# Two more two-level products in layer one's first down stage and one in layer two's, and evictions moved to ScalarE and GpSimd

## The chip, the cores and the metric

The kernel runs on one core of one Trainium2 chip. The metric is the time of one execution on the device in microseconds (us). The median of three runs of the kernel before is 1431.98 us.

## The reference: what is computed

An input `x` of 2048 tokens by 1024 features in bf16 passes through two blocks, twice with the same weights:

```python
x = x + A(layernorm(x), wqkv, wo)                 # linear attention, 32 heads
x = x + B(layernorm(x), w_gate, w_up, w_down)     # ((x @ w_gate) * (x @ w_up)) @ w_down
x = x + A(layernorm(x), wqkv, wo)
x = x + B(layernorm(x), w_gate, w_up, w_down)
```

`w_gate` and `w_up` are 1024x3584, `w_down` is 3584x1024. One A and one B together are a layer here: layer one and layer two. The change concerns the last product of B, by `w_down`.

## The kernel before, in words

**Order of work.** The program is recorded first: each operation goes into a list with the memory that it reads and writes, and each engine then runs its own operations in the order in which they were recorded. Waits between engines come from the memory they share. All transfers are issued by SyncE (SP) from one queue, in recorded order too. So an operation that waits holds up everything recorded behind it on its engine. SBUF is one big tensor named `arena`, PSUM is one named `ps`; that is why all rows read `arena<-ps` and the like.

**Block B** runs in two passes (`ps_` 0 and 1) of 1024 tokens. A pass has a gate/up stage, which leaves h in SBUF, and a down stage (`down`), in which h (1024x3584) is multiplied by `w_down` (3584x1024). The down stage is a Strassen-Winograd product: seven products, named "1" to "7", each of 512 tokens by 1792 by 512, in the order that `DPROD` gives, over sums of blocks of h and of `w_down`.

**One-level product** (matmuls L2109): four token tiles `t`, each with 14 matmuls of 512 columns into one PSUM bank, then the eviction of that bank. In a stage of layer one's first pass VectorE also prepares sums of weight blocks there, one quarter a tile.

**Two-level product** (`two_level`, matmuls L2017): the same scheme once more inside the product, seven sub-products (1, 5, 6, 7, 2, 3, 4 in order of time) of 7 matmuls of 256 columns for each of two token halves, 98 matmuls. Beside the matmuls it needs
- token sums: `a_sums` makes four sums of blocks of h, each 128x1792 on VectorE (three into a buffer, one in place);
- weight sums: `r_sums` makes four sums of weight blocks, 128x1792 each, in layer one's first pass; they are stored in DRAM (`d_scratch`) and loaded again in the later passes;
- seeds (L2021): ScalarE copies a partial product from one PSUM bank to another, where later sub-products add to it;
- a copy into SBUF of sub-product 5 on ScalarE (L2035), and joins (L2024) in which VectorE adds that copy to another partial product in PSUM.

The table `DTWO` says which products of a pass run at two levels: before, none in layer one's first pass, 5, 3 and 2 in layer two's first, and 5, 3, 2 and 4 in the second pass of both.

**Fillers.** `EX` is a list of sums for the next two-level product, from which `ex_pop` records a few at fixed places; `x_pop` does the same with sums of x and of weights for the next gate/up stage (T1 to T4, each 2048 wide, are four of them); `ring_issue` issues the next weight load; `stash` stores rows of x in DRAM to free their place, and they are loaded again later. `pro_step` records, inside product 3, the first matmuls (L1668, L1593) of the stage that follows.

**Evictions.** `stt` (L844) is VectorE's scaled add of a PSUM bank and a term in SBUF; `tt` (L841) is VectorE's sum of two SBUF operands; `evict_x` lets ScalarE copy the bank to SBUF, scaled (L2060), and GpSimd add the rest (L2062). `evict5` is the eviction of product 5, two terms a tile. In layer two `final` issues the output transfer of a finished piece.

## Time and profile before

| | us |
|---|---|
| runs, lowest to highest (three) | 1431.52 to 1432.1 |
| median | 1431.98 |
| profiled execution | 1432.3 |
| its span, first to last instruction | 1430.6 |
| TensorE busy | 1420.2 |
| VectorE, ScalarE, GpSimd busy | 1167.1, 733.5, 314.6 |
| down stages of layer one, passes 0 and 1, about | 403 to 488, 651 to 730 |
| down stages of layer two, passes 0 and 1, about | 1108 to 1191, 1348 to 1428 |

The granted TensorE clock is full speed throughout. A row of the timeline gives start, duration, engine, line, operation, tensors, shape, how many instructions are put together, and in brackets the idle time before with what ended it. A row of the groups ends with the busy time in us and the mean in ns of one instruction. A row of the windows gives a stretch of time, and for each engine the busy time and the number of instructions.

### The profile page before, as it was taken

Reading aid. Unit: us, or ns where it says so; the run is one execution under the profiler, and the core shown is the slowest. Engines: PE = TensorE matmul, PEld = TensorE weight load, DVE = VectorE, ACT = ScalarE, POOL = GpSimd, SP = SyncE. Lnnn points to the kernel's source line nnn. Section 1 sums busy time; section 2 is a strip of 40 time slices with the busy share of each in tenths; the row PEclk is TensorE's granted clock in tenths of the full one; section 3 lists DMA queues with packets and bytes.
Section 4 is the critical chain, followed back from the end, with each engine's and each line's share of the span. In section 5 each row is a group of like instructions: output and inputs, shape, how many; then the busy total and the mean of one; then the engine's idle time right before and its main releaser. Section 6 shows DMA issues by size and latency. Waiting matters only on the chain.

```text
span 1430.6 us, 22386 instructions
## 1 busy us (share of the span) xinstructions
PE 1420.2 (99%) x8332; PEld 809.8 (57%) x8388; DVE 1167.1 (82%) x2012; ACT 733.5 (51%) x1538; POOL 314.6 (22%) x321
## 2 busy tenths in 40 slices
PE   9999999999999999999999999999999999999999
PEld 4444444555544555554764444456666477666658
DVE  7878887888879799878778878779877877777886
ACT  4752367767621255552256523667776116777521
POOL 5644632000013000003334346301000400000160
PEclk9999999999999999999999999999999999999999
DMA  6316867987878899985998067589976699788668
GB/s 235 106 28 182 182 137 195 289 294 251 290 253 286 296 324 303 293 260 171 262 355 220 27 178 162 137 229 273 287 253 200 224 299 317 255 261 265 207 187 259
DMA packets 393997, 330.15 MB, mean 231 GB/s; under 512 B 178337, under 2 KB 342049, under 8 KB 393377
## 3 DMA queue, kind: packets, MB, share of 16 engines
q1 hardware_dynamic: 393888, 328.72, 77.0%
q8 instruction: 66, 1.08, 0.3%
q14 instruction: 43, 0.34, 0.1%
HBM read 238.49 MB, written 66.58 MB: 213 GB/s over the span
## 4 chain that ended last, share of the span: by engine, by line
PE 95%; DVE 2%; ACT 1%; issue 1%; POOL 1%; DMA 0%; SPq 0%; ACTq 0%
PE ps L1593 27%; PE ps L1668 18%; PE ps L2109 14%; PE ps L2017 8%; PE ps L1499 8%; PE ps L1401 8%; PE ps L1167 6%; PE ps L971 4%; PE ps L981 2%; PE ps L1413 1%; ACT arena L493 0%; DVE arena L841 0%; DMA arena<-in_A_x_dram 0%; PE ps L1441 0%; ACT arena L473 0%
## 5 line engine op out<-in xcount | busy, mean ns | idle before, releaser
L841 DVE TENSOR_TENSOR arena<-arena 128x512 f16<-128x512 f16 (+9 forms) x780 | 480.5, 644 | 76.4 <-ACT arena L1712 45.1
L1593 PE MATMUL ps<-arena 128*128 128x512 f16 x1808 | 446.8, 379 | 0.6 <-ACT ps L1623 0.6
L1668 PE MATMUL ps<-arena 128*128 128x256 f16 x2324 | 312.1, 273 | 0.7 <-ACT arena L1712 0.6
L844 DVE SCALAR_TENSOR_TENSOR arena<-ps,arena 128x512 f16<-128x512 f32 (+2 forms) x392 | 259.9, 685 | 38.8 <-PE ps L1593 16.3
L1668 PEld LDWEIGHTS ps<-arena 128*128 128x128 f16 (+1 forms) x2324 | 226.4, 98 | 104.0 <-DVE ps L1687 3.8
L1593 PEld LDWEIGHTS ps<-arena 128*128 128x128 f16 (+1 forms) x1808 | 176.5, 98 | 141.7 <-ACT ps L1623 1.1
L2062 POOL TENSOR_TENSOR arena<-arena 128x512 f32<-128x512 f32 x56 | 87.4, 1565 | 596.5 <-ACT arena L2060 591.5
L2109 PE MATMUL ps<-arena 128*128 128x512 f16 (+1 forms) x941 | 205.7, 379 | 0.6
L1598 ACT ACTIVATE arena<-ps 128x512 f16<-128x512 f32 x224 | 134.0, 598 | 91.8 <-PE ps L1593 89.8
L2109 PEld LDWEIGHTS ps<-arena 128*128 128x128 f16 x952 | 93.2, 98 | 111.5
L1684 ACT COPY ps<-ps 128x256 f32<-128x256 f32 x220 | 81.0, 368 | 79.8 <-PE ps L1668 73.4
L1687 DVE TENSOR_TENSOR ps<-ps,arena 128x256 f32<-128x256 f32 x220 | 92.3, 428 | 34.5 <-PE ps L1668 18.3
L2017 PE MATMUL ps<-arena 128*128 128x256 f16 (+1 forms) x1078 | 119.0, 273 | 0.1
L1401 PE MATMUL ps<-arena 128*128 128x512 bf16 x499 | 114.1, 379 | 0.7
L2017 PEld LDWEIGHTS ps<-arena 128*128 128x128 f16 x1078 | 104.9, 98 | 13.9 <-DVE ps L2024 0.4
L1499 PE MATMUL ps<-arena 128*128 128x512 bf16 x500 | 110.7, 379 | 0.6
L2060 ACT ACTIVATE arena<-ps 128x512 f32<-128x512 f32 x48 | 28.7, 597 | 132.6 <-PE ps L2109 132.6
L1167 PE MATMUL ps<-arena 128*128 128x512 bf16 (+1 forms) x412 | 94.7, 379 | 0.8 <-DVE ps L1171 0.3
L1307 POOL TENSOR_TENSOR arena<-arena 128x1024 f16<-128x1024 f32 x32 | 80.0, 2501 | 69.5 <-DVE arena L1305 62.3
L1623 ACT COPY ps<-ps 128x512 f32<-128x512 f32 x112 | 64.2, 573 | 50.2 <-PE ps L1668 44.8
L1006 POOL TENSOR_TENSOR arena<-arena 128x512 f32<-128x512 f32 x60 | 73.6, 1245 | 69.4 <-DVE arena L1096 33.6
L1499 PEld LDWEIGHTS ps<-arena 128*128 128x128 f16 x512 | 50.1, 98 | 59.8
(80 smaller groups left out, 1262.0 us busy)
## 6 DMA issues: line engine op xcount, KB each, us to landing
arena<-w_scratch SPq DMA_DIRECT2D x84, 512.0 KB, 5.2
arena<-sp_scratch SPq DMA_DIRECT2D x56, 512.0 KB, 5.8
arena<-t_scratch SPq DMA_DIRECT2D x27, 896.0 KB, 5.8
arena<-in_B_w_down_dram SPq DMA_DIRECT2D x18, 896.0 KB, 6.2
w_scratch<-arena SPq DMA_DIRECT2D x28, 512.0 KB, 6.0
sp_scratch<-arena SPq DMA_DIRECT2D x28, 512.0 KB, 4.4
arena<-in_B_w_gate_dram SPq DMA_DIRECT2D x42, 256.0 KB, 5.1
arena<-in_B_w_up_dram SPq DMA_DIRECT2D x42, 256.0 KB, 3.4
```

Source lines behind the costliest of these rows:

```text
L841: P.add("dve", lambda e: e.tensor_tensor(out=out, in0=a, in1=b, op=op), rd=rd, wr=wr, prd=prd)
L844: P.add("dve", lambda e: e.scalar_tensor_tensor(out=out, in0=a, scalar=sc, in1=b, op0=ALU.mult, op1=op1), rd=rd, wr=wr, prd=prd)
L1167: P.add("pe", lambda e: [e.matmul(psb(bank), x[:, k, :], w[:, k, :], start=(start and k == 0), stop=(k == 3), skip_group_check=True) for k ...
L1401: return [e.matmul(psb(bank), xr[:, t, j * 128:(j + 1) * 128], pk[:, h, t, :], start=(t == 0), stop=(t == NST - 1)) for t in range(NST)]
L1499: return [e.matmul(psb(bank), xnT[:, g, i * 128:(i + 1) * 128], wp[:, g, dh * 512:(dh + 1) * 512], start=(dh == 0 and g == 0), stop=(g == ...
L1593: P.add("pe", lambda e: [e.matmul(psb(bank), w[:, k, :], x[:, k, :], start=(start and k == 0), stop=(k == 3), skip_group_check=True) for k ...
L1598: P.add("act", lambda e: e.activation(t, psb(bank), AF.Copy, scale=SG), prd=[bank], wr=r)
L1668: P.add("pe", lambda e: [e.matmul(psb(bank)[:, 256 * half:256 * half + 256], w[:, k, :], xx[:, k, :], start=(start and k == 0), stop=(k == ...
L1687: P.add("dve", lambda e: e.tensor_tensor(out=psb(dst[c])[:, 256:512], in0=lo, in1=c5, op=ALU.add), prd=[bk], rd=rc5, pwr=[dst[c]])
L2017: P.add("pe", lambda e: [e.matmul(psb(bank)[:, 256 * half:256 * half + 256], a[:, k, :], w[:, k, :], start=(start and k == 0), stop=(k == ...
L2062: P.add("pool", (lambda k2, x: lambda e: e.tensor_tensor(out=rtmp[k2], in0=rtmp[k], in1=x, op=ALU.add))(k2, x), rd=rx + rr(k), wr=rr(k2))
L2109: return [e.matmul(psb(bank), hv[:, 7 * hf + k, t * 128:(t + 1) * 128], w[:, k, :], start=(start and hf == 0 and k == 0), stop=(hf == 1 an ...
```

## The change

- In layer one's first pass products 5 and 3 run at two levels too (`l2j`). Their seven weight operands come straight from the loaded weights and from the sums that `r_sums` makes at the time. For product 5 all the sums but one weight sum (which is put into product 4) are recorded inside product 6; those for product 3 inside product 5. The fourth token sum of each goes to GpSimd.
- In layer two's first pass product 4 runs at two levels; the order of products becomes 1672453, as in the second passes. The fillers T1 to T4 move to products 2 and 4, ahead of the others.
- `evict5` (all four passes) was two VectorE operations a tile. It is now one ScalarE copy out of PSUM and two GpSimd adds.
- In layer one's first pass the third of VectorE's three evictions of product 6 becomes ScalarE's and GpSimd's.
- The sums in DRAM are stored in three parts and laid out contiguously; rows 8 to 15 of x are stashed rather than 11 to 15, to make room.

```diff
-        DPROD = {(True, 0): "1274653", (True, 1): "1672453", (False, 0): "1674253", (False, 1): "1672453"}
-        DTWO = {(True, 0): "", (True, 1): L2D, (False, 0): "532", (False, 1): L2D}
+        DPROD = {(True, 0): "1274653", (True, 1): "1672453", (False, 0): "1672453", (False, 1): "1672453"}
+        DTWO = {(True, 0): "", (True, 1): L2D, (False, 0): L2D, (False, 1): L2D}
...
-                ts = zip([("t1", t1), ("t2", t2), ("t3", t3), ("t4", t4)], has("1"))
-                return [x for a in ts for x in a] + has("3") + has("2") + has("5")
+                return [("t1", t1), ("t2", t2), ("t3", t3), ("t4", t4)] + has("1") + has("3") + has("2") + has("5")
...
+                l2j = "53" if first and ps_ == 0 else ""
...
+                            lambda: op(blk[1, 0], blk[0, 0], blk[1, 0], ALU.subtract, "pool" if l2j else "dve")]
...
                 def evict5(t, bank):
-                    pb = psb(bank)
                     xs, rx = xq(1, 1, t)
-                    stt(xs, pb, CD, rtmp[r11 + t], rr(r11 + t), rx, prd=[bank])
+                    o = (O_XN[0] if t == 3 else RE + 2048 * t) if l2j else o_rt[t]
+                    u, ru = vf(o, 512), R(o, 2048)
+                    P.add("act", lambda e: e.activation(u, psb(bank), AF.Copy, scale=CD), prd=[bank], wr=ru)
+                    P.add("pool", lambda e: e.tensor_tensor(out=rtmp[4 + t], in0=rtmp[4 + t], in1=u, op=ALU.add), rd=ru + rr(4 + t), wr=rr(4 + t))
+                    P.add("pool", lambda e: e.tensor_tensor(out=xs, in0=rtmp[r11 + t], in1=u, op=ALU.add), rd=ru + rr(r11 + t), wr=rx)
                     final(1, 1, t)
-                    stt(rtmp[4 + t], pb, CD, rtmp[4 + t], rr(4 + t), rr(4 + t), prd=[bank])
...
                         if q != "3" and i in (1, 5, 7, 2):
-                            ex_pop(1)
+                            ex_pop(2 if l2j else 1)
...
-                    if q in l2d:
-                        ex_pop(4)
-                        nq = {"2": "4" if four else "5", "4": "5", "5": "3"}.get(q)
-                        if nq:
+                    if q in l2d + l2j:
+                        ex_pop(8)
+                        nq = {"2": "4", "4": "5", "5": "3"}.get(q)
+                        if nq and l2j:
+                            (ops, store), a_ = r_sums(nq), a_sums(nq)
+                            EX.extend([a_[0], ops[0], lambda a_=a_, ops=ops: [a_[3](), ops[1]()], a_[1], ops[2], ops[3], a_[2]])
+                            SQ.append(store)
+                        elif nq:
                             EX.extend(a_sums(nq))
...
+                        if q == "4" and t == 3:
+                            r5, store = r_sums("5")
+                            r5[0]()
+                            SQ.append(store)
+                        if q == "6":
+                            if t == 0:
+                                a_, r5 = a_sums("5"), r_sums("5")[0]
+                                EX.extend([a_[0], lambda a_=a_: [a_[3](), r5[1]()], r5[2], a_[1], r5[3], a_[2]])
+                            ex_pop([1, 2, 1, 2][t])
...
-                            xs, rx = xq(0, 1, t)
-                            stt(rtmp[4 + t], pb, CD, xs, rx, rr(4 + t), prd=[bank])
                             stt(rtmp[t], pb, CD, rtmp[t], rr(t), rr(t), prd=[bank])
+                            evict_x(t, bank, 4 + t, (4 + t, xq(0, 1, t)))
...
-                elif not first and q in "453":
-                    x_pop({"4": [2, 2, 2, 2], "5": [0, 0, 0, 1], "3": [1, 2, 3, 3]}[q][t])
+                elif not first and q in "2453":
+                    x_pop({"2": [0, 1, 0, 1], "4": [0, 1, 0, 1], "5": [1, 1, 1, 1], "3": [2, 3, 3, 3]}[q][t])
```

Three places where the order of instructions changes. In these listings a row is a line of the program, the operation, its tensors and shape, what it waits for (s_ an engine, d_ a transfer), and how many follow one another. Line numbers of the changed kernel are a little higher.

**Layer one's first pass, products 4, 6, 5 and 3.** ScalarE before, from the last evictions of the one-level products to the next stage's copies:

```order
L2060 ACTIVATE arena<-ps 128x512 [waits s_pe] x12
L1684 COPY ps<-ps 128x256 [waits s_pe]
L1694 COPY arena<-ps 128x256
L1623 COPY ps<-ps 128x512 [waits s_pe]
L1684 COPY ps<-ps 128x256 [waits s_pe] x2
```

ScalarE now (L2090 are the evictions, the last four being those of product 6; L2048 and L2062 are the seeds and copies of a two-level product; L1986 is the new `evict5`):

```order
L2090 ACTIVATE arena<-ps 128x512 [waits s_pe] x12
L2090 ACTIVATE arena<-ps 128x512 [waits s_dve] x4
L2048 COPY ps<-ps 128x256 [waits s_act,s_pe] x2
L2062 COPY arena<-ps 128x256 [waits s_pe] x2
L2048 COPY ps<-ps 128x256 [waits s_pe] x2
L1986 ACTIVATE arena<-ps 128x512 [waits s_pe] x4
```

VectorE now, from the last of product 6's evictions (L851) to product 5's first joins (L2051); L1933 is a token sum, L848 a weight sum:

```order
L848 TENSOR_TENSOR arena<-arena 128x1792 [waits d_xs14,s_dve]
L1933 TENSOR_TENSOR arena<-arena 128x1792 [waits s_dve]
L851 SCALAR_TENSOR_TENSOR arena<-ps,arena 128x512 [waits s_pool,s_pe]
L851 SCALAR_TENSOR_TENSOR arena<-ps,arena 128x512
L1933 TENSOR_TENSOR arena<-arena 128x1792
L848 TENSOR_TENSOR arena<-arena 128x7x256 [waits d_rr1,d_dw0]
L848 TENSOR_TENSOR arena<-arena 128x7x256 [waits d_dw1,d_rr2]
L1933 TENSOR_TENSOR arena<-arena 128x1792 [waits s_dve]
L2051 TENSOR_TENSOR ps<-ps,arena 128x256 [waits s_pe] x2
```

Before, ScalarE had nothing to do in products 6, 5 and 3 until the next stage's copies. Now four evictions that wait for VectorE stand directly ahead of the seeds of product 5, and on VectorE two sums stand ahead of the last evictions and four between these and the first joins.

**Layer two's first pass, products 5 and 3.** SP before, from the last load of `w_down` on:

```order
L441 DMA arena<-in_B_w_down_dram 128x7x512 [waits s_pe]
L441 DMA out_dram<-arena 128x512 [waits s_dve] x2
L441 DMA arena<-d_scratch 128x7x256
L441 DMA out_dram<-arena 128x512 [waits s_dve] x2
L441 DMA arena<-in_B_w_gate_dram 128x4x128
L441 DMA arena<-in_B_w_gate_dram 128x4x256
```

SP now:

```order
L441 DMA arena<-in_B_w_down_dram 128x7x512 [waits s_pe]
L441 DMA arena<-sp_scratch 128x4x512
L441 DMA out_dram<-arena 128x512 [waits s_pool] x2
L441 DMA arena<-d_scratch 128x1792
L441 DMA out_dram<-arena 128x512 [waits s_pool] x2
L441 DMA arena<-in_B_w_gate_dram 128x4x128
L441 DMA arena<-in_B_w_gate_dram 128x4x256
```

The output transfers of product 5 stood behind VectorE and now stand behind GpSimd; the first gate weights of the next stage are behind them, as before.

**The same place on VectorE**, now, around product 3's joins (L848 with 512 or 2x256 are fillers of `x_pop`):

```order
L848 TENSOR_TENSOR arena<-arena 128x2x256
L848 TENSOR_TENSOR arena<-arena 128x512 [waits s_dve]
L848 TENSOR_TENSOR arena<-arena 128x512 [waits s_pool]
L848 TENSOR_TENSOR arena<-arena 128x512 [waits s_dve]
L2051 TENSOR_TENSOR ps<-ps,arena 128x256 [waits s_pe] x2
L2051 TENSOR_TENSOR ps<-ps,arena 128x256 [waits s_act] x2
```

Before, the eight evictions of product 5 (the last two are shown) and two fillers stood there; the evictions' s_pool is for sums of the one-level products, and the fillers wait for no GpSimd:

```order
L844 SCALAR_TENSOR_TENSOR arena<-ps,arena 128x512 [waits s_pool,s_pe]
L844 SCALAR_TENSOR_TENSOR arena<-ps,arena 128x512
L841 TENSOR_TENSOR arena<-arena 128x512
L841 TENSOR_TENSOR arena<-arena 128x512 [waits s_dve]
L2024 TENSOR_TENSOR ps<-ps,arena 128x256 [waits s_pe] x2
L2024 TENSOR_TENSOR ps<-ps,arena 128x256 [waits s_act] x2
```

A filler that waits for GpSimd now stands ahead of the joins.

More of the change, by code (lines that the diff above doesn't have):

```diff
@@ L1868, in tail @@
                         ring_issue()
[L1869 removed]
+                    for t in range(0 if ps_ else 1 if jit else 3, 8):
                         i = 8 * ps_ + t
@@ L2185, in dticks0 @@
                 if q == ("2" if first else "1") and t == 3:
-                    for k in range(5):
-                        stash(11 + k)
-                if q == "4" and t < 2 and not first:
+                    for k in range(8, 16):
+                        stash(k)
+                if q == "5" and t < 2 and not first:
                     sp_load(1, t, "12")
@@ L2205, in ticks1 @@
             def ticks1(u):
-                if first and u == 3:
-                    SQ.pop(0)()
                 if u % 4 < 2 and not is_last and nxt.t_next < 8:
```

104 lines of the change are left out of this document (56 added, 48 removed).

## The prediction

> **What bounds the kernel now.** I read the chain of waits first, to see which engine ends last; then the groups, for prices; then the windows over the down passes, to see what stands free there.
>
> ```profile
> PE 1420.2 (99%) x8332; PEld 809.8 (57%) x8388; DVE 1167.1 (82%) x2012; ACT 733.5 (51%) x1538; POOL 314.6 (22%) x321
> PE 95%; DVE 2%; ACT 1%; issue 1%; POOL 1%; DMA 0%; SPq 0%; ACTq 0%
> L2109 PE MATMUL ps<-arena 128*128 128x512 f16 (+1 forms) x941 | 205.7, 379 | 0.6
> L2017 PE MATMUL ps<-arena 128*128 128x256 f16 (+1 forms) x1078 | 119.0, 273 | 0.1
> L2062 POOL TENSOR_TENSOR arena<-arena 128x512 f32<-128x512 f32 x56 | 87.4, 1565 | 596.5 <-ACT arena L2060 591.5
> L1307 POOL TENSOR_TENSOR arena<-arena 128x1024 f16<-128x1024 f32 x32 | 80.0, 2501 | 69.5 <-DVE arena L1305 62.3
> ```
>
> TensorE is the bound, and its matmuls in the down stages wait for nothing (0.6 and 0.1 us idle over the whole program). So a matmul that goes saves its time in full, and a wait that comes saves nothing and costs its full length. The question is whether VectorE, ScalarE, GpSimd and SP's queue keep their work behind TensorE. The windows over layer one's first down pass (403 to 488 us; here products 4, 6 and 5), with the busy time of PE, PEld, DVE, ACT and POOL, say how much cover is left:
>
> ```profile
> 439.00:451.00 12.00, 12.00 (x57) 5.42 (x56) 12.00 (x10) 2.39 (x4) 6.40 (x4) 1.00 0.60 227
> 451.00:463.00 12.00, 12.00 (x57) 5.46 (x56) 10.53 (x15) 0.60 (x1) 1.28 (x1) 1.00 0.89 301
> 463.00:475.00 12.00, 12.00 (x58) 5.40 (x57) 8.14 (x10) 0.00 (x0) 0.00 (x0) 1.00 0.50 153
> ```
>
> VectorE has none in product 4, 1.5 us in product 6 and 3.9 us in product 5. It is a second bound there.
>
> **A, the matmuls saved.** A one-level product is 4 token tiles of 14 matmuls; ScalarE's evictions in it and, in a two-level product, ScalarE's first seed copies give the periods:
>
> ```profile
> 445.19 0.60 ACT L2060 ACTIVATE arena<-ps 128x512 f32<-128x512 f32 x1 [2.42 <-PE ps L2109]
> 448.21 0.60 ACT L2060 ACTIVATE arena<-ps 128x512 f32<-128x512 f32 x1 [2.42 <-PE ps L2109]
> 451.23 0.60 ACT L2060 ACTIVATE arena<-ps 128x512 f32<-128x512 f32 x1 [2.42 <-PE ps L2109]
> 1168.67 0.36 ACT L2021 COPY ps<-ps 128x256 f32<-128x256 f32 x1 [4.99 <-PE ps L2017]
> 1179.37 0.36 ACT L2021 COPY ps<-ps 128x256 f32<-128x256 f32 x1 [4.99 <-PE ps L2017]
> ```
>
> 3.02 x 4 = 12.08 us against 10.70 us: 1.38 us a product, for three products (5 and 3 of layer one, 4 of layer two) **-4.1 us**. The groups give a bound from the other side: 205.7/17 = 12.10 and 119.0/11 = 10.82, so -3.8.
>
> **B, VectorE in layer one's first pass.** VectorE's stretches there:
>
> ```profile
> 433.10 22.70 DVE L841 TENSOR_TENSOR arena<-arena 128x1792 f16<-128x1792 f16 x18 [0.64 <-PE ps L2109]
> 455.73 3.92 DVE L844 SCALAR_TENSOR_TENSOR arena<-ps,arena 128x512 bf16<-128x512 f32 x6
> 463.32 2.02 DVE L844 SCALAR_TENSOR_TENSOR arena<-ps,arena 128x512 bf16<-128x512 f32 x3 [1.01 <-PE ps L2109]
> ```
>
> Product 4's matmuls end at 451.2, but VectorE comes to product 6's evictions only at 455.7. The two-level product 5 now needs, inside product 6, four weight sums and three token sums (each 1792 wide; the fourth token sum is GpSimd's), with one weight sum more in product 4. The adds have two prices, by window, type and shape:
>
> ```profile
> L841 DVE TENSOR_TENSOR arena<-arena 128x1792 f16<-128x1792 f16 x7 | 11.2, 1629 | 0.0
> L2062 POOL TENSOR_TENSOR arena<-arena 128x512 f32<-128x512 f32 x4 | 6.1, 1522 | 5.7 <-ACT arena L2060 5.7
> ...
> L841 DVE TENSOR_TENSOR arena<-arena 128x1792 f16<-128x1792 f16 x4 | 4.3, 1084 | 0.0
> L844 DVE SCALAR_TENSOR_TENSOR arena<-ps,arena 128x512 bf16<-128x512 f32 x4 | 2.8, 692 | 2.6 <-PE ps L2109 2.5
> L2062 POOL TENSOR_TENSOR arena<-arena x56: 1147/1470/2043, 406.6 to 1389.0; 128x512 f32<-128x512 f32 x56
> ...
> 1174.75 2.08 DVE L841 TENSOR_TENSOR arena<-arena 128x1792 f16<-128x1792 f16 x2
> 1176.75 4.87 DVE L844 SCALAR_TENSOR_TENSOR arena<-ps,arena 128x512 bf16<-128x512 f32 x8
> ```
>
> From 443.3 to 454.2 us, beside four GpSimd adds, a wide add takes 1.63 us; from 464 to 472.5, with GpSimd idle, 1.08. GpSimd's own add goes from 1.15 (its minimum) to 1.52. So VectorE loses 7 x 0.545 = 3.8 us to GpSimd work that alone would be 4 x 1.15 = 4.6 us: 0.83 us for each. Back to back two adds start 2.0 us apart from what follows (1174.75 to 1176.75), and eight evictions take 4.87 us, 0.61 each, with or without GpSimd.
>
> The sum: with 1.08 us more in product 4, VectorE is at product 6 at 456.8. It has 6 wide adds at 1.0 and 8 evictions at 0.61 to do, 10.9 us, and is done at 467.7 if GpSimd costs it nothing. ScalarE's four evictions of product 6 each wait for VectorE (first listing of the order), and behind the fourth stand product 5's seed copies. Its first sub-product can run (1.5 us), the second waits for the seeds. Product 5 would have begun at 463.3, so its second sub-product at 464.8; now it is 467.7 + 0.6 + 0.6 = 468.9. **The stall is 4.1 us.** Four more wide adds (two token sums and two weight sums for product 3) then stand on VectorE ahead of product 5's first join, which comes 3.1 us after the seed copy:
>
> ```profile
> 1171.73 0.43 DVE L2024 TENSOR_TENSOR ps<-ps,arena 128x256 f32<-128x256 f32 x1 [1.01 <-PE ps L2017]
> ```
>
> Seeds at 468.3, join at 471.4; the adds end at 467.7 + 4.0 = 471.7: 0.3 more, 4.4 in all if GpSimd costs nothing. But GpSimd has four adds and one 1792 wide in product 6 (the wide one estimated from L1307 at 2.5 x 1.75 = 4.4 us): 9 us of work, of which a little over half meets an add rather than an eviction. At 0.83 that is 3.8 us, the last eviction ends at 471.5 and the stall is 7.9. In product 5 the next wide GpSimd add begins behind the first of the four, so one takes 1.0 and three 1.63: they end at 477.4, against a join at 472.1 + 3.1 = 475.2, 2.2 us more. I take **+10.1 us**, nearest to the row with GpSimd at work; ends 4.4 and 13, the upper if each GpSimd microsecond is lost in full. That the third VectorE eviction of product 6 goes to ScalarE and GpSimd is in the count (8 for 12).
>
> [...]
>
> **C, token sums in layer two's first pass.** Four 2048-wide adds (T1 to T4) move from one-level products to the two-level 2 and 4, two in each, between VectorE's last join of one and the first of the next:
>
> ```profile
> L841 DVE TENSOR_TENSOR arena<-arena 128x2048 f16<-128x2048 f16 x1 | 1.2, 1216 | 0.0
> ```
>
> VectorE stands idle 1.0 us ahead of such a join (row of 1171.73). Two adds at 1.15 from start to start are 2.3, less 1.0 of idle: 1.3 a product, **+2.4 us** for two (0.8 if TensorE has half a microsecond to spare each time, 3.5 with GpSimd beside it).
>
> **D, SP's queue at the end of that pass.** Product 5's eviction is now one ScalarE copy and two GpSimd adds a tile, eight adds in a row. The output transfers wait for GpSimd, and the next gate/up stage's first weights stand behind them in SP's queue (second listing).
>
> ```profile
> 1181.62 1.58 SPq L441 DMA_DIRECT2D arena<-in_B_w_gate_dram  x2
> 1186.94 0.60 PE L1668 MATMUL ps<-arena 128*128 128x256 f16 x4
> arena<-in_B_w_gate_dram SPq DMA_DIRECT2D x42, 128.0 KB, 5.3
> arena<-in_B_w_gate_dram SPq DMA_DIRECT2D x42, 256.0 KB, 5.1
> ```
>
> Before, VectorE's eight evictions took 1176.75 to 1181.6, the weights were issued at 1181.62, and 1181.62 + 5.3 = 1186.9 is just when the next stage's first matmuls run, inside product 3. Now ScalarE copies first (0.6 us), then eight adds at 1.15 to 1.57 us: done at 1177.3 + 9.2 = 1186.5 to 1189.9, and the issue comes at 1187 to 1190, 5.5 to 8.5 us late. With no slack that is the stall. Inside it falls a VectorE add that waits for the sixth GpSimd add and stands ahead of product 3's joins (third listing; 1.5 to 3 us, not added). I take **+6.5 us**, ends 5 and 9.
>
> **E, the rest.** The last pass evicts product 5 the same way, and its last outputs and the reload of product 3's weight sums stand behind GpSimd: 0 to +2, I take +0.6 (the end is product 3's, 10.7 us later). SP's row stash in layer one waits for GpSimd too: 0 to +1, I take +0.5. The smaller VectorE load of passes 1 gains nothing, since TensorE doesn't wait there; the smaller reload and the other layout of the sums likewise.
>
> **Sum:** -4.1 + 10.1 + 2.4 + 6.5 + 0.6 + 0.5 = +16.0 us on the profiled execution's 1432.3 (a span of 1430.6 and 1.7 around it), 1448.3. That execution is 0.3 over the median of the runs, so **1448.0 us**. All terms at their lower ends: -4.1 + 4.4 + 0.8 + 5 = +6.1, 1438; at their upper: -3.8 + 13 + 3.5 + 9 + 2 + 1 = +24.7, 1456.
>
> **Rivals.** First, **all of it hidden**: 1432.0 - 4.1 = 1427.9, faster. For it speaks that VectorE is 82% busy over the program and GpSimd 22%, and that products 5 and 3 in the pass 1 of each layer already run at two levels without waits. Against it stands the row of 455.73: VectorE is 4.5 us behind before anything is added. Chance 0.10.
>
> Second, **only layer one stalls**: the gate weights aren't needed as early as the row of 1186.94 lets it seem, so D falls to the 1.5 us of the VectorE wait and the rest stays: 1448.0 - 5.0 = 1443; with GpSimd costing VectorE nothing besides, 1443 - 5.7 = 1437. Chance 0.25 together. If C is hidden as well and B is at its lower end, the loss shrinks to about the gain: -4.1 + 4.4 = +0.3, the same time as before, 1432.3. Chance 0.06.
>
> Third, **GpSimd holds VectorE up in full**. The 1792-wide GpSimd add starts right after the sum it depends on; if VectorE's next add waits out all 4.4 us of it, and of each small add what it doesn't spend in evictions, product 6 costs 2 us more than I took and product 5 another 1: 1448 + 3 = 1451, and with D at its upper end 1453.5. Chance 0.14. It decides wherever two VectorE adds stand next to one another beside a GpSimd add.
>
> The forecast itself has 0.45. A measurement of this kernel tells 0.2%, 2.9 us, from no change. Faster by more: the first rival, 0.10. Within it: 0.06. Slower: 0.45 + 0.25 + 0.14 = 0.84. The likeliest case alone spans 1441 to 1454; the range takes in most of the second rival and the bounds of the costs, **1435 to 1456**.
>
> **What would show it.** A: L2044 (the two-level matmul's new line) with 1372 matmuls, seed copies of products 5 and 3 of layer one 10.7 us apart but for the stalls. B: TensorE idle near 465 us for 4 to 10 us, ended by the seed copy on ScalarE or the join on VectorE; VectorE at once after its last eviction of product 6 near 468 to 472. C: idle time of 1 us or so ahead of the first joins of products 4 and 5 of layer two's first pass. D: SP's gate load issued 5 to 8 us later against product 3's first seed, and TensorE idle until it lands. I am wrong if TensorE's sum stays within 1 us of its span there: then VectorE had slack that I have not seen, most likely because GpSimd's adds fall into its evictions.

## The result

The changed kernel takes 1454.5 us (median of four runs, 1452.9 to 1455.0) against 1432.0 us before: 22.5 us slower, a ratio of 1.0153 with a 95% interval of 1.0135 to 1.017. The prediction was 1448, with a range of 1435 to 1456.

The page of the changed kernel, busy times and then the chain of waits:

```profile
PE 1427.0 (98%) x8514; PEld 824.5 (57%) x8514; DVE 1176.6 (81%) x2002; ACT 751.7 (52%) x1576; POOL 379.4 (26%) x363
PE 87%; DVE 7%; DMA 2%; issue 1%; SPq 1%; ACT 1%; POOL 1%; DVEq 0%
```

TensorE's share of the chain falls from 95% to 87%, VectorE's rises from 2% to 7%. The groups of the matmuls show that what was to be saved was saved, and that idle time has come in (the last field is the idle time ahead of the group):

```profile
L2044 PE MATMUL ps<-arena 128*128 128x256 f16 (+1 forms) x1372 | 159.0, 279 | 16.9 <-DVE ps L2051 9.0
L2138 PE MATMUL ps<-arena 128*128 128x512 f16 (+1 forms) x784 | 170.0, 379 | 0.0
```

1372 matmuls are 14 two-level products, 784 are 14 one-level products: three have changed sides. The two-level products now wait 16.9 us, where it was 0.1.

The first and last matmul of each down stage, read from both timelines:

| stage | before | changed | difference |
|---|---|---|---|
| layer one, pass 0 | 402.9 to 488.8 | 403.1 to 502.0 | +13.0 |
| until the next | 157.0 | 157.9 | +0.9 |
| layer one, pass 1 | 645.8 to 730.2 | 659.9 to 744.5 | +0.2 |
| layer two, pass 0 | 1108.6 to 1190.6 | 1122.7 to 1213.2 | +8.5 |
| layer two, pass 1 | 1348.7 to 1427.7 | 1371.1 to 1450.3 | +0.2 |
| after the last matmul | 2.9 | 2.9 | 0 |

The few tenths left are the stretches between and before. The spans are 1430.6 and 1453.2: all of the 22.6 us is in the two first passes and just behind the first.

### The profile page after: what moved, and what is told of

Its sections match the earlier page's. It is cut to its first block, busy times and chain, and to the rows that moved or that the text cites. A ratio compares the mean times of both kernels' runs of the same rounds, so it can differ in the third digit from the quotient of the medians.

```text
span 1453.2 us, 22808 instructions
## 1 busy us (share of the span) xinstructions
PE 1427.0 (98%) x8514; PEld 824.5 (57%) x8514; DVE 1176.6 (81%) x2002; ACT 751.7 (52%) x1576; POOL 379.4 (26%) x363
## 4 chain that ended last, share of the span: by engine, by line
PE 87%; DVE 7%; DMA 2%; issue 1%; SPq 1%; ACT 1%; POOL 1%; DVEq 0%
PE ps L1599 24%; PE ps L1674 17%; PE ps L2138 10%; PE ps L2044 9%; PE ps L1407 8%; PE ps L1505 6%; PE ps L1173 6%; PE ps L977 5%; DVE arena L848 4%; PE ps L987 3%; DMA arena<-in_B_w_down_dram 1%; DVE arena L1933 1%; DVE arena L851 1%; SPq L441 1%; PE ps L1419 0%
## 5 line engine op out<-in xcount | busy, mean ns | idle before, releaser
L848 DVE TENSOR_TENSOR arena<-arena 128x512 f16<-128x512 f16 (+8 forms) x736 | 432.8, 616 | 84.7 <-ACT arena L1718 45.5
L851 DVE SCALAR_TENSOR_TENSOR arena<-ps,arena 128x512 f16<-128x512 f32 (+1 forms) x360 | 239.5, 685 | 25.7 <-PE ps L1599 16.3
L2092 POOL TENSOR_TENSOR arena<-arena 128x512 f32<-128x512 f32 x64 | 103.7, 1631 | 567.8 <-ACT arena L2090 305.6
L2044 PE MATMUL ps<-arena 128*128 128x256 f16 (+1 forms) x1372 | 159.0, 279 | 16.9 <-DVE ps L2051 9.0
L2138 PE MATMUL ps<-arena 128*128 128x512 f16 (+1 forms) x784 | 170.0, 379 | 0.0
L2044 PEld LDWEIGHTS ps<-arena 128*128 128x128 f16 x1372 | 136.6, 100 | 38.6 <-DVE ps L2051 10.1
L2138 PEld LDWEIGHTS ps<-arena 128*128 128x128 f16 x784 | 76.7, 98 | 92.5
L2090 ACT ACTIVATE arena<-ps 128x512 f32<-128x512 f32 x52 | 31.1, 597 | 150.7 <-PE ps L2138 132.6
L1012 POOL TENSOR_TENSOR arena<-arena 128x512 f32<-128x512 f32 x60 | 73.6, 1246 | 69.4 <-DVE arena L1102 33.6
L1505 PEld LDWEIGHTS ps<-arena 128*128 128x128 f16 x512 | 50.1, 98 | 59.8
```

What stands on the lines that cost most here:

```text
L848: P.add("dve", lambda e: e.tensor_tensor(out=out, in0=a, in1=b, op=op), rd=rd, wr=wr, prd=prd)
L851: P.add("dve", lambda e: e.scalar_tensor_tensor(out=out, in0=a, scalar=sc, in1=b, op0=ALU.mult, op1=op1), rd=rd, wr=wr, prd=prd)
L1505: return [e.matmul(psb(bank), xnT[:, g, i * 128:(i + 1) * 128], wp[:, g, dh * 512:(dh + 1) * 512], start=(dh == 0 and g == 0), stop=(g == ...
L2044: P.add("pe", lambda e: [e.matmul(psb(bank)[:, 256 * half:256 * half + 256], a[:, k, :], w[:, k, :], start=(start and k == 0), stop=(k == ...
L2092: P.add("pool", (lambda k2, x: lambda e: e.tensor_tensor(out=rtmp[k2], in0=rtmp[k], in1=x, op=ALU.add))(k2, x), rd=rx + rr(k), wr=rr(k2))
L2138: return [e.matmul(psb(bank), hv[:, 7 * hf + k, t * 128:(t + 1) * 128], w[:, k, :], start=(start and hf == 0 and k == 0), stop=(hf == 1 an ...
```

## Layer one's first pass, after

TensorE's timeline:

```profile
463.55 1.69 PE L2044 MATMUL ps<-arena 128*128 128x256 f16 x14
473.11 5.58 PE L2044 MATMUL ps<-arena 128*128 128x256 f16 x28 [7.86 <-ACT ps L2048]
480.88 16.36 PE L2044 MATMUL ps<-arena 128*128 128x256 f16 x133 [2.20 <-DVE ps L2051]
...
498.36 0.39 PE L1674 MATMUL ps<-arena 128*128 128x256 f16 x2 [0.90 <-DVE arena L848]
```

Product 5's first sub-product ran (14 matmuls), then TensorE waited 7.86 us for the seeds and later 2.20 us for a join. VectorE and GpSimd in the same stretch:

```profile
457.16 1.08 DVE L1933 TENSOR_TENSOR arena<-arena 128x1792 f16<-128x1792 f16 x1
...
463.52 3.27 DVE L1933 TENSOR_TENSOR arena<-arena 128x1792 f16<-128x1792 f16 x1
...
470.87 1.28 DVE L851 SCALAR_TENSOR_TENSOR arena<-ps,arena 128x512 bf16<-128x512 f32 x2
...
473.07 2.03 DVE L848 TENSOR_TENSOR arena<-arena 128x1792 f16<-128x1792 bf16 x1
475.02 4.45 DVE L848 TENSOR_TENSOR arena<-arena 128x1792 f16<-128x1792 bf16 x1
479.40 1.08 DVE L1933 TENSOR_TENSOR arena<-arena 128x1792 f16<-128x1792 f16 x1
```

```profile
461.42 4.43 POOL L1933 TENSOR_TENSOR arena<-arena 128x1792 f16<-128x1792 f16 x1
...
472.85 1.30 POOL L2092 TENSOR_TENSOR arena<-arena 128x512 f32<-128x512 f32 x1 [2.85 <-ACT arena L2090]
474.12 4.42 POOL L1933 TENSOR_TENSOR arena<-arena 128x1792 f16<-128x1792 f16 x1
```

VectorE ends product 6's evictions at 472.15, ScalarE's copy and the seeds follow, and TensorE goes on at 473.1. Look at the two adds from 473.07; with GpSimd idle an add of this width takes 1.08 us, as at 479.40. The first meets a short GpSimd add, which ends at 474.15, and ends itself at 475.10; the second meets the long one, which ends at 478.54, and ends itself at 479.47. So each ends 0.93 to 0.95 us after the GpSimd add that it meets, and the long one costs it 3.4 us. The add of 3.27 us at 463.52 does the same: GpSimd's add ends at 465.85, it at 466.79.

The windows show something that no row of the kernel before has. The last three numbers of such a row are the granted clock, the share of the DMA engines and GB/s:

```profile
474.00:476.00 2.00, 2.00 (x11) 1.40 (x10) 2.00 (x2) 0.37 (x1) 2.00 (x2) 0.50 1.14 366
486.00:488.00 2.00, 2.00 (x20) 1.80 (x19) 1.60 (x2) 1.19 (x2) 0.75 (x1) 1.00 0.00 0
```

Behind the idle time of 7.86 us the clock is 0.50, and it stays there for 4.8 us of work: 11 matmuls in 2 us from 474, where 20 go at full clock from 486. The last section has the moments at which it changes.

## Layer two's first pass, after

TensorE, then VectorE, GpSimd and SP, at the join of product 3:

```profile
1175.25 10.87 PE L2044 MATMUL ps<-arena 128*128 128x256 f16 x98 [0.64 <-DVE ps L2051]
1187.33 10.87 PE L2044 MATMUL ps<-arena 128*128 128x256 f16 x98 [1.20 <-DVE ps L2051]
1203.13 6.55 PE L2044 MATMUL ps<-arena 128*128 128x256 f16 x35 [4.92 <-DVE ps L2051]
1209.51 0.60 PE L1674 MATMUL ps<-arena 128*128 128x256 f16 x4
```

```profile
1199.86 2.87 DVE L848 TENSOR_TENSOR arena<-arena 128x512 f16<-128x512 f16 x2 [4.82 <-POOL arena L1988]
```

```profile
1192.04 1.31 POOL L1987 TENSOR_TENSOR arena<-arena 128x512 f32<-128x512 f32 x1 [27.76 <-ACT arena L1986]
...
1198.57 1.26 POOL L1988 TENSOR_TENSOR arena<-arena 128x512 bf16<-128x512 f32 x1
```

```profile
1202.85 1.04 SPq L441 DMA_DIRECT2D arena<-in_B_w_gate_dram  x2
```

The first joins of products 4 and 5 come 0.64 and 1.20 us late; the one of product 3 comes 4.92 us late, because a filler on VectorE waits for GpSimd's sixth add (the one at 1198.57) and stands ahead of it. The gate weights are issued at 1202.85, but the next stage's first matmuls, at 1209.51, have no wait of their own: by then the weights are there.

## Where the 22.6 us are

Layer one, +13.0: two products' matmuls, -2.8; the three waits, 7.86 + 2.20 + 0.90 = +11.0; the rest, +4.8, is the slow clock for the most part (28 matmuls in 5.58 and 133 in 16.36 us; with the clock kept up, in a run below, 3.23 and 14.69: 4.0 us). Layer two, +8.5: -1.4, the waits +6.8, and the rest +3.1, of which 2.6 are the 35 matmuls in 6.55 us that take 4.00 us in a run without the long wait. Of the +0.9 behind layer one's stage the rows give 0.48: a filler on VectorE waits for a late weight load, and TensorE for the eviction behind that filler.

```profile
520.52 1.55 DVE L848 TENSOR_TENSOR arena<-arena 128x512 f16<-128x512 bf16 x4 [1.62 <-DMA arena<-in_B_w_up_dram]
522.73 1.04 PE L1599 MATMUL ps<-arena 128*128 128x512 f16 x4 [0.48 <-DVE arena L851]
```

With product 5's eviction back on VectorE (a run below) that stretch takes 157.2 us instead of 157.9. Then there is +0.2 in each second pass, and some tenths elsewhere. In the two first passes about 1.3 us stay without a row.

## Experiments

All ratios are against the kernel before, run on the same chip (1432.4 to 1432.7 us). The interval of a ratio is some 2 us to either side, so a difference of 1 or 2 us between two of these kernels is read from their traces.

### The fourth token sums back on VectorE

```diff
-        op(blk[1, 0], blk[0, 0], blk[1, 0], ALU.subtract, "pool" if l2j else "dve")
+        op(blk[1, 0], blk[0, 0], blk[1, 0], ALU.subtract, "dve")
```

> The changed kernel with the fourth token sum of layer one's products 5 and 3 on VectorE again; nothing is left out. Theory (GpSimd's 4.4 us add holds VectorE's next add up for as long as it runs): in the changed kernel one add took 3.27 us at 463.5 and two took 6.41 us at 473.1, against 1.0 each; without the GpSimd adds VectorE loses one add of 1.0 us in each product and wins 3.2 and 4.4, so the seed wait falls from 7.9 to about 5.7 us and the join wait of 2.2 goes: 1449 to 1450.5 us. Rival (the sheer number of VectorE's adds sets the stall): two adds more, 1456 to 1457 us.

1447.2 us, ratio 1.0104 (1.0089 to 1.0119): 7.3 us faster than the change, with two adds more on VectorE. TensorE's timeline:

```profile
469.59 20.63 PE L2044 MATMUL ps<-arena 128*128 128x256 f16 x161 [4.75 <-ACT ps L2048]
```

The seed wait is 4.75 us and the join wait is gone. That is more than was expected: the seed wait is 1 us shorter than the 5.7 expected, and there is one slow stretch of the clock in place of two (its mean is 0.74 over 463 to 475 us and 0.98 over 475 to 488, where the change has 0.70 and 0.76). The rival, that the number of adds sets the stall, falls; it is GpSimd's long add that holds VectorE up. The 4.75 us that stay are VectorE's own backlog, near the 4.1 us that the prediction worked out for a GpSimd that costs nothing. For in this kernel the holding goes the other way: in product 6 VectorE's adds take 1.07 us each, and GpSimd's short adds, 1.30 us in the change's row of 472.85, take up to 5.31 us beside them.

```profile
469.33 5.31 POOL L2092 TENSOR_TENSOR arena<-arena 128x512 f32<-128x512 f32 x1 [0.89 <-ACT arena L2090]
```

### ScalarE's evictions of product 6 freed from VectorE

```diff
+        P.add("act", lambda e: e.activation(u, pb, AF.Copy, scale=CD), prd=[bank], wr=ru)   # u: another buffer
         stt(xs, pb, CD, rtmp[4 + t], rr(4 + t), rx, prd=[bank])
         stt(rtmp[t], pb, CD, rtmp[t], rr(t), rr(t), prd=[bank])
-        evict_x(t, bank, 4 + t, (4 + t, xq(0, 1, t)))
+        P.add("pool", lambda e: e.tensor_tensor(out=rtmp[4 + t], in0=u, in1=xo, op=ALU.add), rd=ro + ru, wr=rr(4 + t))
```

> The changed kernel with ScalarE's evictions of layer one's product 6 put ahead of VectorE's and into another buffer, so that they wait for TensorE alone; nothing is left out. Theory (VectorE's backlog sets the stall, ScalarE's queue only shows it): the seeds come about 4.5 us earlier, when VectorE has freed the banks they go to, but the joins still wait for VectorE, near 480 us; the idle time moves from the seeds to the joins: 1452.5 to 1455 us. Rival (the order on ScalarE's queue is the cause): 4.5 us of idle time and a part of the slow stretch behind it go: 1447 to 1450 us.

1455.9 us, ratio 1.0163 (1.0148 to 1.0179), as slow as the change.

```profile
466.54 0.94 PE L2044 MATMUL ps<-arena 128*128 128x256 f16 x7 [1.86 <-ACT ps L2048]
469.32 4.66 PE L2044 MATMUL ps<-arena 128*128 128x256 f16 x21 [1.84 <-ACT ps L2048]
480.96 16.75 PE L2044 MATMUL ps<-arena 128*128 128x256 f16 x133 [6.98 <-DVE ps L2051]
```

The seeds come earlier, and the third stretch still starts at 481: the idle time has gone to the joins. ScalarE's queue, which stands in the row of the 7.86 us wait, was not the cause; VectorE's work ahead of the joins was.

### TensorE kept busy during the waits

Matmuls that do nothing for the result, into a bank that a seed overwrites later, behind sub-products 1 and 6 of layer one's product 5. First with 70 and 21:

```diff
+        if l2j and q == "5" and i in (1, 6):
+            (fa, fra), (fw, frw) = lhs(1, 0), W[1]
+            for _ in range(10 if i == 1 else 3):
+                P.add("pe", 7 matmuls of fa by fw into bank dst[2])
```

> The changed kernel with 91 more matmuls in layer one's product 5, 70 behind its first sub-product and 21 behind its third, into a bank that is written over afterwards; the result is not touched. They fill the time in which TensorE waits. Theory (TensorE's clock falls because it stood idle, and the slow matmuls behind the wait are a loss of their own of 4 to 5 us): the clock stays near 1.0, the waits are as long as before: 1449 to 1451 us. Rival (the slow stretch has another cause than the idle time, such as memory traffic): 1454 to 1457 us.

1455.2 us, ratio 1.0157 (1.0142 to 1.0172). The clock stayed up (1.00 over 463 to 475 us) and the 28 matmuls took 3.23 us instead of 5.58, but the second group read an operand whose place a weight load for the next stage overwrites, and waited 3.5 us for that load; what was won was lost again.

```profile
478.63 3.98 PE L2083 MATMUL ps<-arena 128*128 128x256 f16 x21 [3.47 <-DMA arena<-in_B_w_up_dram]
```

So once more, with `W[2]` in place of `W[1]` and 42 in place of 21:

> As the kernel with 91 more matmuls, but with 70 and 42, and with operands that no later transfer overwrites (the 21 matmuls of the first version waited 3.5 us for such a transfer). They are to keep TensorE busy until the joins. Theory (the clock falls because of idle time; VectorE finishes the sums ahead of the joins near 480.4 us whatever TensorE does, so only the slow matmuls behind the joins can be won, 16.4 against 14.7 us): 1452.3 to 1453.7 us. Rival (nothing to be won, the matmuls that fill cost their own time): 1454.5 to 1457 us.

1453.2 us, ratio 1.0143 (1.0129 to 1.0156), 1.3 us below the change, which is within the intervals; the rows decide. TensorE's timeline (L2083 are the matmuls that fill):

```profile
464.39 7.80 PE L2083 MATMUL ps<-arena 128*128 128x256 f16 x70
472.42 3.23 PE L2044 MATMUL ps<-arena 128*128 128x256 f16 x28 [0.22 <-ACT ps L2048]
475.48 4.75 PE L2083 MATMUL ps<-arena 128*128 128x256 f16 x42
480.20 14.69 PE L2044 MATMUL ps<-arena 128*128 128x256 f16 x133
```

This gives two results. The slow matmuls come from the idle time: with TensorE busy the granted clock is 1.00 from 463 to 490 us, and the 28 take 3.23 us instead of 5.58. And of the slow stretch's 4.0 us in layer one only the part behind the joins, 16.36 less 14.69, is a loss of the clock's own; the 2.35 us ahead of them lie under VectorE's backlog, which ends near 480 us either way. Without the slow clock the join wait would have been about 4.55 us, not 2.20: the 28 matmuls end at 475.65 here, and those behind the joins start at 480.20.

### Idle time alone, in the kernel before

A row of ScalarE copies ahead of product 5's first matmul in layer one's first pass, seven and fourteen of them:

```diff
+        P.add("act", lambda e: e.activation(u, psb(B_DX[3]), AF.Copy, scale=CD), prd=[B_DX[3]], wr=hold)
+        for _ in range(6):                                  # 13 in the longer one
+            P.add("act", lambda e: e.activation(u, u, AF.Copy, scale=CD), rd=hold, wr=hold)
...
-        P.add("pe", fn, rd=rw + ..., pwr=[bank])
+        P.add("pe", fn, rd=rw + ... + hold, pwr=[bank])     # the first matmuls only
```

> The kernel before with seven ScalarE copies of some 0.6 us in a row ahead of product 5's first matmul in layer one's first pass, so that TensorE stands idle for about 4.3 us; nothing else changes, and nothing is left out. Theory (idle time of this length makes the clock fall, and the matmuls behind it lose 2.5 to 3 us more, as behind the 4.9 us wait of the changed kernel): 1439 to 1440.5 us. Rival (the slow matmuls there had another cause): 1436.4 to 1437.2 us.

> As the one with seven copies, but with fourteen, an idle time of about 8.5 us. Theory (the slow stretch has a fixed length once the clock has fallen): 1443.2 to 1444.7 us, about 2.5 to 3 us over the idle time again. Rival (the loss grows with the idle time): 1446 us or more. Rival (no loss from the clock): 1440.6 to 1441.4 us.

1441.4 us (ratio 1.0062, 1.0047 to 1.0077) and 1446.4 us (1.0097, 1.0082 to 1.0112). The copies took longer than reckoned; the idle times were 6.70 and 11.33 us:

```profile
469.49 19.72 PE L2115 MATMUL ps<-arena 128*128 128x512 f16 x76 [6.70 <-ACT arena L2107]
```

```profile
474.36 15.93 PE L2115 MATMUL ps<-arena 128*128 128x512 f16 x60 [11.33 <-ACT arena L2107]
```

Over the idle time the kernel lost 8.9 - 6.7 = 2.2 us and 13.9 - 11.3 = 2.6 us. So the figures expected in us were missed because of the length of the stall (1446.4 us is where a rival had it, but for a stall of 8.5 us), while the loss behind it is about as expected and does not grow with it. Each of these differences has an uncertainty of some 2 us, so it is the traces that carry this point. There layer one's first down stage takes 95.7 and 100.0 us instead of 85.9, which is 3.1 and 2.8 us more than the idle time, and no other down stage has changed. The windows of the shorter and the longer stall:

```profile
463.00:468.00 5.00, 0.00 (x0) 0.00 (x0) 2.80 (x4) 3.00 (x5) 0.00 (x0) 0.72 1.07 320
474.00:476.00 2.00, 2.00 (x7) 0.76 (x6) 0.35 (x1) 0.00 (x0) 0.00 (x0) 0.64 0.00 0
```

```profile
463.00:468.00 5.00, 0.03 (x1) 0.00 (x0) 2.98 (x4) 2.76 (x5) 0.00 (x0) 0.80 1.07 310
478.00:480.00 2.00, 2.00 (x7) 0.71 (x6) 0.00 (x0) 0.00 (x0) 0.00 (x0) 0.59 0.00 0
```

A mean of 0.72 over 463 to 468 is full clock until 465.2 and half from there, 2.4 us after the idle time began at 462.8; 0.64 over 474 to 476 is half clock until 475.4, 6.0 us after the matmuls came back at 469.5. In the longer stall the same reading gives 3.0 and 5.3 us. At half clock 6 matmuls go in 2 us, where 11 go at full clock. So 6.0 and 5.3 us of it lose about half of that, 3.0 and 2.6 us, which is what the stages lost.

### Product 5's eviction back on VectorE

```diff
-        P.add("act", ...); P.add("pool", ...); P.add("pool", ...)       # evict5, as changed
+        stt(xs, pb, CD, rtmp[r11 + t], rr(r11 + t), rx, prd=[bank])     # evict5, as before
+        stt(rtmp[4 + t], pb, CD, rtmp[4 + t], rr(4 + t), rr(4 + t), prd=[bank])
```

> The changed kernel with product 5's eviction on VectorE again in all four passes (two scaled adds a tile, as before); nothing is left out. Theory (GpSimd's eight adds hold up a filler on VectorE and SP's queue at the end of layer two's first pass): the 4.9 us wait of product 3's joins and the slow stretch of 2.7 us behind it go, and eight evictions of 0.61 us with the fillers ahead of the joins bring about 2 us back: 1447.5 to 1450.5 us. Layer one's waits of 7.9 and 2.2 us stay. Rival (VectorE is so full that taking the evictions back costs what it gives): 1453.5 to 1456 us.

1447.4 us, ratio 1.0103 (1.0088 to 1.0118), 7.1 us faster than the change. In layer two product 3's join waits 0.66 us instead of 4.92 and the matmuls behind it are at full speed:

```profile
1198.02 4.00 PE L2042 MATMUL ps<-arena 128*128 128x256 f16 x35 [0.66 <-DVE ps L2049]
```

The eight VectorE evictions that came back cost less than the 2 us allowed there. Layer one's first pass takes 99.7 us there instead of 98.9. The rival falls.

### The waiting filler moved behind the joins

```diff
-        "3": [2, 3, 3, 3]
+        "3": [0, 5, 3, 3]
```

> The changed kernel with two fillers moved, in layer two's first pass, from ahead of product 3's first joins to behind its second joins, the one that waits for GpSimd among them; nothing is left out. Theory (SP's late gate weights are a second wait behind the first): the 4.9 us wait of the joins goes, but the gate weights, issued at 1202.85 and landing near 1208, are then needed near 1202, so most of it comes back there: 1451.5 to 1454 us. Rival (the VectorE add alone is the cause, the weights have slack): the 4.9 us and the slow stretch behind them go: 1446.5 to 1448.5 us.

1451.5 us, ratio 1.0132 (1.0115 to 1.0149): 2.9 us of a possible 7.5; the intervals of this kernel and of the change overlap, but in the traces the stage takes 87.3 instead of 90.5 us. Product 3's joins wait no more, and in their place:

```profile
1187.58 14.83 PE L2044 MATMUL ps<-arena 128*128 128x256 f16 x133 [1.20 <-DVE ps L2051]
1205.62 1.04 PE L1674 MATMUL ps<-arena 128*128 128x256 f16 x4 [3.21 <-DMA arena<-in_B_w_gate_dram]
1206.45 1.70 PE L2044 MATMUL ps<-arena 128*128 128x256 bf16 x7
```

SP's late gate weights are a second wait, 3.2 us, that the first had hidden, and a slow stretch follows it too (7 matmuls in 1.70 us instead of 0.93). The eviction through GpSimd holds TensorE up in two ways at once, and each hides the other.

### Layer one's first pass as before

```diff
-        l2j = "53" if first and ps_ == 0 else ""
+        l2j = ""
```

and the branches of that pass put back as in the kernel before.

> The changed kernel with layer one's first pass at one level again, as before (products 5 and 3 and product 6's evictions too); the rest of the change stays, and nothing is left out. By the stages of the two traces layer one's first down stage lost 13.0 us, and 0.9 us came after it; layer two's first lost 8.5. Theory (the two losses are independent of one another): 1432.3 + 8.5 = 1440 to 1441.5 us. Rival (the rest of the change costs layer one too, by the moved stash and the new layout): above 1442 us.

1445.6 us, ratio 1.0096 (1.0079 to 1.0113), more than expected. VectorE's timeline says why:

```profile
489.78 1.55 DVE L848 TENSOR_TENSOR arena<-arena 128x512 f16<-128x512 f16 x4 [6.07 <-DMA d_scratch<-arena]
```

The change puts product 5's weight sums where rows 8 and on of x were; with product 5 at one level these sums are made later, and a filler waits until they are stored. With the sums in their old place:

> As the changed kernel with layer one's first pass at one level again, and with the weight sums of product 5 where they were before (with these in the place of x's rows, VectorE waited 6.1 us for their store, and TensorE 4.0 us). Nothing is left out. Theory (layer two's loss of 8.5 us stands alone): 1440 to 1441.5 us. Rival (the moved stash and layout cost layer one something else): above 1442 us.

1440.1 us, ratio 1.0052 (1.0036 to 1.0067): layer two's part of the change (with `evict5` in all passes) costs 7.4 us by itself, layer one's 14.4. Product 3's join waits there as it does in the change:

```profile
1189.49 5.44 PE L2044 MATMUL ps<-arena 128*128 128x256 f16 x35 [4.93 <-DVE ps L2051]
```

The first of the two kernels shows a cost of that place of the sums which the change itself doesn't have, since it makes them earlier.

### Both undone

The fourth token sums and product 5's eviction on VectorE, in one kernel.

> The changed kernel with both undone: the fourth token sums of layer one and product 5's eviction on VectorE again. Nothing is left out. Theory (the two losses lie in different stages and add up, 7.3 and 7.1 us): 1439.3 to 1441 us. Rival (with the evictions of product 5 on VectorE too, layer one's VectorE is late again at product 3): 1442 us or more.

1442.7 us, ratio 1.007 (1.0056 to 1.0084): 11.8 us of the 14.4 that the two give singly. TensorE's waits in this kernel:

```profile
PE ps L2042 <- ACT ps L2046: 4.8, 1, 4.8
PE ps L2042 <- DVE ps L2049: 2.5, 3, 1.2
PE ps L2042 <- DVE arena L851: 0.9, 2, 0.6
```

The 0.9 us for VectorE's evictions of layer one (L851) are of the rival's kind, but small. The 2.6 us that seem to be missing lie within the spread: the four runs differ by 2.8 us among themselves. In the traces the spans are 6.2 and 7.5 us shorter singly and 13.4 us together: there the two losses add up. Even so the kernel is 10 us behind the one before: the seed wait stays.

### Layer two's product 4 alone

Layer one and `evict5` as before, and T1 to T4 moved from products 2 and 4 into 6, 7 and 2:

```diff
-        "2": [0, 1, 0, 1], "4": [0, 1, 0, 1], "5": [1, 1, 1, 1]
+        "6": [0, 0, 0, 1], "7": [0, 1, 0, 1], "2": [0, 1, 0, 1], "4": [0, 0, 1, 0], "5": [0, 1, 0, 1]
```

> Layer one as before and product 5's eviction on VectorE; of the change only layer two's product 4 at two levels is left, with the sums T1 to T4 moved into its one-level products 6 and 7 and one into 2. Nothing is left out. Theory (the matmuls saved, 1.4 us, show once the fillers don't stand ahead of the joins): 1430.8 to 1432.3 us. Rival (VectorE has no room in the one-level products of layer two either, since each add beside GpSimd takes 1.6 us or more): 1432.5 to 1435 us.

1442.2 us, ratio 1.0068 (1.0056 to 1.0081). Contrary to what stands above, something of the computation does change here: T1 to T4 are made in the memory that holds product 7's operand `hE`, the first of them ahead of product 7, so that this product works on other numbers. And for the same reason VectorE stands still until product 7's matmuls have read it:

```profile
1145.87 1.23 DVE L848 TENSOR_TENSOR arena<-arena 128x2048 f16<-128x2048 f16 x1 [7.07 <-PE ps L2136]
```

TensorE in turn waits 5.6 us for these sums. So this says nothing on whether VectorE has room there. It says that the place of T1 to T4 behind product 7 is forced by memory. No kernel among these beats the one before.

## Why the prediction was right, and what it missed

**A, the matmuls saved:** right, three products changed sides.

**B, layer one:** the waits came as worked out: 7.86 us for the seeds where the step had 7.9, and 2.20 us for the join where it had 2.2. The first for the right reason: VectorE was at product 6 at 457.2 (456.8 predicted) and done at 472.15 (471.5), GpSimd cost it 4.1 us there (15.0 for work priced at 10.9) where the step had 3.8, and its backlog is what the run with ScalarE's evictions freed shows to be the cause. The price of 0.83 us for each GpSimd us is a mean, though: it was lost in three whole waits (1.0, 2.2 and 1.0 us). The second is right by accident. The step let three adds take 1.63 us each beside GpSimd's long one and end at 477.4; they ended at 480.5, since one add took 2.03 and one 4.45 us, which is the third rival's mechanism. But the matmuls ahead of the join ran at half clock and reached it 2.35 us later too. A third wait, 0.90 us for a filler ahead of the next stage's first matmuls, was not in the step.

**C:** 2.4 us predicted (twice 1.3 is 2.6), 0.64 + 1.20 measured. Right in the main; the second wait also has a filler of 0.42 us ahead of the join that the step did not count.

**D:** the step failed in its mechanism. It said 6.5 us by SP's queue and let the VectorE filler's wait (1.5 to 3 us) fall inside it. The filler's wait was 4.92 us and came first; SP's, 3.2 us, is seen only when the filler is moved. The weights were issued as late as the step said: 0.7 us after they were needed in that run (1203.12 against 1202.41), where before it was 5.3 us ahead. But the load landed 2.5 us after its issue, not 5.3, and at 5.3 the wait would have been 6.0 us. That the cause is product 5's eviction through GpSimd holds, as its undoing shows.

**E:** 0.9 us behind layer one for 0.5 (SP waits 7.4 us for GpSimd there, which it never does before, and the weight load of the row of 520.52 is late), none at the end for 0.6.

**The missing term.** The sum fell 6.5 us short of the result. Every wait in it was priced at its length. Three of the waits, of 7.86, 2.20 and 4.92 us, cost more: the clock fell to 0.50, and the matmuls behind them ran at half speed for 4.8, 3.4 and 5.3 us. Between measured rows and the full-clock rows of other runs that is 4.0 us in layer one and 2.6 us in layer two. That this makes up the whole gap is in part chance. Of the 4.0 us, 2.35 lie under VectorE's backlog: at full clock B's join wait would have been that much longer. So B was 2.35 us short, the clock's own loss is 1.7 + 2.6 = 4.3 us, and the 0.90 us wait and some 1.3 us without a row come to these; against them C and D were 2.1 us too high. The sentence that a wait "costs its full length" is the one that was wrong. The windows that the prediction shows have a granted clock of 1.00, but in stretches in which TensorE is never idle; they could not show what a wait does to it.

**Rivals.** That all is hidden fell, and so did that only layer one stalls (layer two alone costs 7.4 us). The third, GpSimd holding VectorE up in full, is what happens at the five meetings in this stretch in which GpSimd's add had begun first, beside short ones too, though not where it was priced: VectorE was done with product 6 only 0.65 us later than the step had it (the rival had 2), with the sums of product 5 3.1 us later (the rival had 3 in all), and the slow clock hid 2.35 us of that.

## What to carry to other kernels

Where TensorE is busy 99% of the time and VectorE is already late in a stage, a cheaper product that needs more sums is paid for by VectorE, and handing one of these sums to GpSimd can cost VectorE more than doing it: 7.3 us were won by taking two back. Price a new TensorE wait of 2 us or more at its length and up to 3 us more. That is an estimate from the waits of these runs: beyond its length one of 2.32 us cost 0, one of 2.20 us 1.7, the same one of 4.9 us 1.4 in one kernel and 2.6 in another, and the stalls of 6.7 and 11.3 us about 3. When a wait is found, look for the next one on another queue that it hides, before taking it as the gain.

## What the runs showed of the hardware

**The clock fell behind waits, and in these traces only at certain moments.** Four windows of half a microsecond in the changed kernel, in which the granted clock changes:

```profile
467.50:468.00 0.50, 0.00 (x0) 0.00 (x0) 0.50 (x2) 0.00 (x0) 0.30 (x1) 0.71 0.61 187
477.50:478.00 0.50, 0.50 (x5) 0.32 (x3) 0.50 (x1) 0.00 (x0) 0.50 (x1) 0.55 0.19 43
481.00:481.50 0.50, 0.50 (x5) 0.40 (x4) 0.15 (x1) 0.00 (x0) 0.00 (x0) 0.86 0.00 0
484.50:485.00 0.50, 0.50 (x5) 0.41 (x4) 0.50 (x1) 0.00 (x0) 0.00 (x0) 0.73 0.00 0
```

Read as above, the clock went to 0.50 at 467.71, to 1.00 at 477.95, to 0.50 at 481.36 and to 1.00 at 484.77. These moments are 10.24, 3.41 and 3.41 us apart: three times, once and once 3.41 us. In the two stalls the clock came back 10.2 and 13.6 us after it fell, three and four times 3.41. The next fall in the changed kernel, at 1201.57 in layer two, is 716.80 us behind the last of the four, 210 times 3.413, and the way back there, at 1208.40, is 6.83 us behind that, twice 3.41. So in these traces the clock changes only at points that lie whole multiples of 3.41 us apart. That the cost of a wait depends on where it falls between them is the author's reading of these rows:

- In the change and the two stalls the fall came 2.4 to 3.4 us after TensorE went idle, and the way back 3.9 to 6.0 us after work was back. The wait of 2.20 us from 478.7 to 480.9 was over when the clock fell.
- The same wait of 4.9 us at product 3's join stands in seven of the kernels, and the 35 matmuls behind it took 6.55 us in the change and 5.44 us in the run with layer one as before and the sums in their old place, against 4.00 without such a wait. In the change they had half clock for 5.3 us, and the loss, 2.55 us, is about half of that; by the same half the other run's loss of 1.44 us is an estimated 2.9 us at half clock.
- With layer one as before and the sums still in their new place a wait of 2.32 us cost nothing more than its length; the granted clock is 1.00 from 475 to 503:

```profile
495.14 1.04 PE L1599 MATMUL ps<-arena 128*128 128x512 f16 x4 [2.32 <-ACT arena L1604]
```

Waits of 0.64 and 1.20 us had no such effect: the 98 matmuls behind them took 10.87 us each time, at a granted clock of 1.00. How long TensorE must be idle for the clock to fall, no run here was made to show.

**Adds on VectorE and GpSimd at once.** From 457 to 480 us of the changed kernel a VectorE add of 128x1792 that met a GpSimd add already begun ended 0.93 to 0.95 us after it, at all five such meetings: it took 2.03 or 2.04 us beside a 128x512 add of 1.30 us, and 3.27 and 4.45 us beside 128x1792 ones. GpSimd's add of 128x1792 took 4.42 and 4.43 us, as estimated from the 128x1024 one (4.4), but each time its first us overlaps a VectorE add, so how long it takes alone is not shown. Two of VectorE's evictions of 128x512 took 1.27 us at 462.32 and 1.28 us at 466.71, beside GpSimd's adds of 4.43 and 2.00 us, and 1.28 us at 458.17 with GpSimd idle: no longer beside it.
